# Another order, engine choice and slot choice for the same pieces of a rotary attention and squared-ReLU MLP kernel

## The chip, the cores and the metric

The kernel runs on one core of a Trainium2 chip. The metric is the device time of one execution in microseconds. Three executions of the kernel before took 625.17, 627.04 and 629.34 us, so the median is 627.04 us.

## The reference

There are 4 batches of 8 heads, 576 positions and 64 dimensions per head. Attention with a rotary embedding of q and k is followed by an MLP on 2304 tokens of width 512 with 2048 hidden units, all in float32:

```python
q_rot, k_rot = rotate(q), rotate(k)                 # rotary, halves of 32
scores = scale * np.matmul(q_rot, k_rot.transpose(0, 1, 3, 2))
scores = scores - np.max(scores, axis=-1, keepdims=True)
attn = np.exp(scores)
attn = attn / (np.sum(attn, axis=-1, keepdims=True) + 1e-09)
out = np.matmul(attn, v)                            # then (2304, 512)
h = x @ w_in
g = s * np.maximum(h, 0.0) ** 2 + b
return g @ w_out
```

## The kernel before

**Pieces.** The function `plan` writes the whole kernel down as 2657 pieces, each with the engines that may run it, the pieces it depends on and the buffers that it opens. Heads are handled in 16 pairs (`pr`, 0 to 15), each with nine score tiles of 128 queries by 576 keys (`i`, 0 to 8; tile 8 holds the last 64 queries of both heads). Tokens go through the MLP in nine units of 256 (`u`, 0 to 8); unit 8 collects the tails of all batches.

**The first pairs and unit 0.** Pairs 0 to 3 are computed in float32: `rotate` (three tensor_tensor steps per operand, lines 573 to 577), `qk_T` (PE transposes, lines 748 and 751), `s_pair` (scores, L638), `s_max` (DVE, L662), `s_exp` (ACT), `p_T` (L776), `pv32` (L795). Unit 0 uses float32 weights (`mlp_in0` L889, `mlp_out0` L906).

**The weights.** The host passes w_in and w_out as 64-bit words. Each of 32 blocks is loaded into one of four `x` slots (`load_w`, L419) and made into float32 by `w_sign`, `w_low`, `w_rebias` and `w_join` (lines 383 to 391). `w_gram` (PE, L459) finds their size, and `w_hi` and `w_lo` split them into two float16 halves. No unit above 0 can start before that.

**The other pairs and units.** Pairs 4 to 15 work with q, k and v split in float16 halves; q and k are transposed by DMA (`transpose_qk`). Probabilities are split by `p_a` (ACT, DVE or POOL: `pab<-p,sum`) and `p_b` (DVE, L388), transposed by DMA from the SP queue (`p_t`, L720, and `p_tt`, L724: `pt<-pab`), and multiplied with v in `pv_sum` (PE, L741, 28 matmuls). A unit runs 16 `mlp_in` (L863, 12 matmuls), `mlp_r` (ACT), `g_hi` (ACT or DVE), `g_lo` (DVE or POOL, L881), 32 `mlp_out` (L930, 3 matmuls), two `out_sum` (DVE) and a `store`. Unit 7 runs last.

**What sets the order.** Three strings do. ORDER is the sequence of all 2657 pieces, two characters for each; PICKS gives the engine of each piece that has a choice (S for ACT, V for DVE, G for POOL); SLOTS gives the buffer of each tile. Every engine runs its own pieces in the sequence of ORDER, every DMA is issued by SP in that sequence, and an engine whose next piece isn't ready waits, with all that stands behind it.

```python
order = [64 * DIGITS.index(ORDER[i]) + DIGITS.index(ORDER[i + 1]) for i in range(0, len(ORDER), 2)]
engs, where, at, steps = iter(PICKS), iter(SLOTS), {}, {}
```

The casts of `p_a`, `qk_hi`, `w_hi` and `v_hi` go through one helper (L383 on DVE, L385 on POOL, L391 on ACT), so in the rows they are told apart by their tiles.

Of the kernel before, what the change touches and what calls it, by code (L numbers as in the profile page):

```python
# [35 lines left out]


ORDER = (
    "AJDTAAEBDUAMAKALECDcDdEDDeEEDfEFEGDgANDhAdEAELEMENDiA3ADA5AfAgD_EHEIAEDjDkDlAeAhEJAFAGAHA6ESDpDqD1EKA4DrA9BAAOJjD2JkDsAI"
# [3 lines left out]
    "BOB2BfBPKJFTK6K7KKKCBhBgETBkEtBQBiFUBlBmB4EwLCBnKWKXBwKLKYKRKDKMKEB6LDB3KeCSBcBWLELFBoE4B5FVBdK8B-FhKSBpBjKfB7KTB8FQKgCV"
    "KZKaKbBqKhCBB_KnKvKwCUKiClLGKUKcKoKdKpCTCAKqKVCWKxCnCmCoKjLJKkK9CCKrCpKyLRLKB9KlCDCLCyCNCYLLLMKmCOKsLrEqK-CEKtLSLTLNLsLU"
    "KzLOC1LVCMCPbLbMbObNCZFHK_LHLtEUC0bPbQCbFKLICaLuLaCsCzLWK0LPCtExbRLicdEyEzbScebTCcE0cfcgE1chLjF7CuF-LkCvC2cicjLbLlE-MRCd"
    "CXLmLXLcLQLvCeE_CwLdMSLYC_CFDCDBLZDADDLnMTLeMUckLfCHLgFkbWbYbXbVLwbZbaE8L3KuK1CfF6DML4MEE9ChMVFRLxbgK2L5MFK3MWCiCIbfL0L1"
# [39 lines left out]
PICKS = (
    "GSSGVSGSSGGSGSSGSSGSSGSSGSSGSSGSGVSSGSSGSSGGGVSSGSSGSGVSSGVSVVSGSSVSSGSGGGSVVSGSSVVSVVSGSSGSSGSSVVSSSVVSSSVVSSSVVSSSVVSS"
    "SVVSGVGGSSSVVSGSVVSSGVVSGGVVSGSVVVSSVVSGSVVSGVVVVGVVGSSVSSSSSSSSSVVSSSSSSSSGSSGSSGVSSSVGSSSSVVSGSSSSVSSSSSVGSVSSSSSSSSSS"
    "SSSSSSSSSSSSSGSSSSSSSSGSGSSSSVSSVSVSSSSSSVSSVSSSSSVSSSSSSVVSSVVSSGSVSSVVVVSGVGSVSVVGVSVGVVVVSSVSSSSGVSGVVVSSSSVVSGSVSSSG"
    "SVSGSVSVSSSSSVVSSGVGVSSSVVSVGVSVSVGSVVSVSVVGSGGVVVSSGVVGSSGGGSGGGSVSGGSSGVSGSSGSVVGSGGSGSSSVVSVSGSGSVSGSVSVSSGSGSVSGSVSV"  # L90
    "SGSVSSVSGSVSGVVVVVVSVVVVVGSGSVVGSGSGSVVVGSGVVSGSVVVVGSVVVVSGVVVGVGSGSGSVVVVVGSGSGSGVVSGVVVSVSGVVSVVVSVVGSG"
)

SLOTS = (
    "000000111002311010000101010123100311110201012001011010030201001203001132100331100112100101013011020103032311001100310210"
    "021010011110010011013212203345120010103100300010001012211511001301013041010001122301100203010011311011500120012103001103"
    "041321001101134012011301202201030100011131301100110540021002011101132305121011011010020102030013011040250100300111121301"
    "100101330112303100041101050101020001234210115013100111230100014101005310120012100301010510020101121120101120310100104522"
    "301100001101110011020210011231100000421031012101103013101140101300223110002111102203023000103110031110050011020010402100"
    "010031110001312001150200410301310211021201011500011131200104020111110500030131010010112031001310141010252130000001121033"  # L100
    "021301001140111000215201110003310411113020031051112010102204001113112101211021300010025010301201402310000110131401100503"
    "011120131321100300420101013151120022014121100301010101120321011020201101001240021001110201113021001300151022201101302100"
    "1041110021010100001312104013100011001021010101013111010210100001112000010012000"
)


# [948 lines left out]
```

## Time and profile before

| what | value |
|---|---|
| median of three executions | 627.04 us |
| the profiled execution's own time | 627.53 us |
| its span, first to last instruction | 625.7 us |
| PE busy | 588.8 us, 94% of the span |
| DVE, ACT, POOL busy | 470.6, 407.3, 123.8 us |
| DMA queue 1 | 89.54 MB, 63.5% of 16 engines |

Busy time is the union of an engine's instructions. Durations of matmuls overlap, as the next one starts before the last has drained: three `mlp_out` matmuls last 0.81 us, and the next work starts 0.65 us after their beginning.

### The profile page before, as it was taken

The numbers are of one execution on the slowest core, as the hardware profiler recorded it, in microseconds if no ns is written. First come the engines' busy times: TensorE is split into PE (matmuls) and PEld (weight loads), VectorE is DVE, ScalarE is ACT, GpSimd is POOL, SyncE is SP. The second block draws the span as 40 slices with busy tenths as digits, with TensorE's granted clock in tenths as the row PEclk, the third lists the DMA queues.
The fourth block names the chain that finished last, engine by engine and source line by source line (L and its number), as shares of the span: only waits on it lengthen the run. The fifth ranks groups of instructions, "written<-read, shape, count | busy, mean of one in ns | idle before, by whom it ended". The sixth has DMA issues, their size and how long they took to land.

```text
span 625.7 us, 12358 instructions
## 1 busy us (share of the span) xinstructions
PE 588.8 (94%) x4634; PEld 396.5 (63%) x4634; DVE 470.6 (75%) x1029; ACT 407.3 (65%) x858; POOL 123.8 (20%) x127
## 2 busy tenths in 40 slices
...
GB/s 282 262 296 200 234 229 243 130 205 171 205 139 104 103 164 224 140 197 174 132 156 142 115 148 144 168 186 134 136 119 65 21 71 40 109 76 39 35 1 34
DMA packets 209868, 90.32 MB, mean 144 GB/s; under 512 B 192272, under 2 KB 196496, under 8 KB 209808
## 3 DMA queue, kind: packets, MB, share of 16 engines
q1 hardware_dynamic: 209808, 89.54, 63.5%
...
q14 instruction: 24, 0.20, 0.1%
...
## 4 chain that ended last, share of the span: by engine, by line
PE 73%; DMA 10%; DVE 7%; ACT 3%; issue 3%; SPq 2%; POOL 1%; DVEq 0%; ACTq 0%; POOLq 0%
PE px L863 25%; PE po L930 24%; PE px L741 8%; PE s L656 7%; DMA pt<-pab 5%; PE po L906 2%; PE px L889 2%; PE s L638 2%; DVE s L662 2%; DMA x<-in_moe_w_in_dram 2%; DMA x<-in_moe_w_out_dram 2%; DVE wio L388 1%; DMA qkT<-nat 1%; PE s L657 1%; ACT x L391 1%
## 5 line engine op out<-in xcount | busy, mean ns | idle before, releaser
L930 PE MATMUL po<-wio,g 128*128 128x512 f16 x768 | 185.5, 379 | 0.0
L863 PE MATMUL px<-xa,wio 128*128 128x256 f16 x1536 | 181.8, 273 | 0.0
L863 PEld LDWEIGHTS <-wio 128*128 128x128 f16 x1536 | 148.3, 98 | 32.8 <-issue 1.3
L391 ACT ACTIVATE p<-s,nm 128x576 f32<-128x576 f32 x144 | 105.6, 734 | 71.5 <-DVE s L662 50.8
L388 DVE SCALAR_TENSOR_TENSOR pab<-p,sum,pab 128x576 f16<-128x576 f32 x136 | 112.0, 839 | 7.3 <-POOL pab L385 4.9
L930 PEld LDWEIGHTS <-g 128*128 128x128 f16 x768 | 70.2, 98 | 73.3 <-issue 4.7
L662 DVE TENSOR_SCALAR_CACHE_REDUCE s<-s,sc 128x576 f32<-128x576 f32 x108 | 87.7, 820 | 24.7 <-PE s L657 22.3
L391 ACT ACTIVATE hr<-px,xc 128x512 f32<-128x512 f32 x64 | 43.6, 682 | 72.4 <-PE px L863 70.9
L881 POOL TENSOR_TENSOR g<-hr,g 128x512 f16<-128x512 f32 x31 | 39.0, 1257 | 189.5 <-ACT g L391 100.2
L391 ACT ACTIVATE pab<-p,sum 128x576 f16<-128x576 f32 x75 | 56.2, 766 | 9.8 <-DVE sum L690 8.0
L741 PE MATMUL px<-pt,v 128*64 128x320 f16 (+2 forms) x640 | 52.0, 281 | 7.2 <-DMA pt<-pab 6.7
L765 DVE CAST g<-hr 128x512 f16<-128x512 f32 x22 | 9.4, 428 | 51.2 <-ACT hr L391 48.2
L385 POOL TENSOR_SCALAR pab<-p,sum 128x576 f16<-128x576 f32 x26 | 23.4, 902 | 123.2 <-DVE sum L690 70.4
L741 PEld LDWEIGHTS <-v 128*64 128x64 f16 x640 | 35.6, 109 | 18.7 <-issue 13.0
L391 ACT ACTIVATE hr<-hr 128x512 f32<-128x512 f32 x68 | 42.7, 628 | 1.5
L656 PE MATMUL s<-qkT 128*128 128x512 f16 (+1 forms) x120 | 41.4, 383 | 0.0
L656 PE MATMUL s<-kS,qkT 128*128 128x512 f16 (+1 forms) x120 | 41.3, 380 | 0.0
L656 PEld LDWEIGHTS <-qkT 128*128 128x128 f16 (+1 forms) x240 | 21.9, 100 | 25.1 <-issue 5.0
L385 POOL TENSOR_SCALAR wio<-x 128x512 bf16<-128x512 f32 (+1 forms) x27 | 22.9, 859 | 54.5 <-ACT x L391 23.7
L889 PE MATMUL px<-x,wio 128*128 128x128 f32 x256 | 32.3, 279 | 0.0
L889 PEld LDWEIGHTS px<-x,wio 128*128 128x128 f32 x256 | 30.0, 192 | 3.1 <-issue 2.2
L662 DVE TENSOR_SCALAR_CACHE_REDUCE s<-s 128x576 f32<-128x576 f32 x36 | 26.8, 766 | 6.1 <-PE s L638 6.1
...
## 6 DMA issues: line engine op xcount, KB each, us to landing
...
```

What stands on the lines that cost most here:

```text
L385: eng.tensor_scalar(out=out, in0=in0, scalar1=s1, scalar2=s2, op0=op0, op1=op1)
L388: nc.vector.scalar_tensor_tensor(out=out, in0=in0, scalar=scalar, in1=in1, op0=op0, op1=op1)
L391: nc.scalar.activation(out=out, in_=in_, func=func, **kw)
L638: nc.tensor.matmul(ps[h][:, to], d["qF"][hh, t * P:(t + 1) * P], d["kF"][hh, keys], start=True, stop=True)
L656: nc.tensor.matmul(ps[rows, MAIN:2 * MAIN], lhs, kk[:, h:8:2], start=(n == 0), stop=(n == 1))
L662: nc.vector.tensor_scalar(out=T["s"], in0=T["s"], scalar1=-1.0 / 8.0 if pr in FQ else st[pr]["es"], scalar2=None, op0=ALU.mult, op1=ALU.mi ...
L741: nc.tensor.matmul(o[64 * h:64 * h + 64, c], v_rows(pr, h, k, z), p_rows(pr, 2 * (i // 4) + h)[:, k, c], start=((z, k) == todo[0]), stop=( ...
L863: nc.tensor.matmul(ph, w16[0][:, f, wz, cc], X["xa"][:, xz, c], start=(c == 0 and n == 0), stop=(c == NC - 1 and n == 2))
L881: (nc.vector if eng == DVE else nc.gpsimd).tensor_tensor(out=g[:, 1], in0=r, in1=g[:, 0], op=ALU.subtract)
L889: nc.tensor.matmul(ph, wi[:, f + 1, c * P:(c + 1) * P], xs[0]["x"][:, c, j * P:(j + 1) * P], start=(c == 0), stop=(c == NC - 1))
L906: nc.tensor.matmul(X["po"][:, j * DM:(j + 1) * DM], gs["h", j, f - f % 4][:, f % 4 * P:(f % 4 + 1) * P], wo[:, f + 1], start=(n == 1), sto ...
L930: nc.tensor.matmul(po, g[:, gz, jj], w16[1][:, f, wz], start=(n == 1 and i == 0), stop=(n == NF and i == 2))
```

## The change

The pieces, their dependencies and the code that emits them stay. ORDER, PICKS and SLOTS are replaced as a whole by strings of the same lengths, which come from a second search at a lower temperature that drew four sets of transfer delays at a time.

```diff
 ORDER = (
-    "AJDTAAEBDUAMAKALECDcDdEDDeEEDfEFEGDgANDhAdEAELEMENDiA3ADA5AfAgD_EHEIAEDjDkDlAeAhEJAFAGAHA6ESDpDqD1EKA4DrA9BAAOJjD2JkDsAI"
+    "AADTEBADDUEAD_AJDcDdECDEEDDeDfEFDiDgELDhEMAEEIENAFAMDjALA3AKANAdDkDlJjAGA5EJAHAfA6AeDrDpAgDsJkAhEGA4JlA9DqEHEKA7DtJrJsJt"
...
-    "GSSGVSGSSGGSGSSGSSGSSGSSGSSGSSGSGVSSGSSVSSGGGVSSGSSGSGVSSGVSVVSGSSVSSGSGGGSVVSGSSVVSVVSGSSGSSGSSVVSSSVVSSSVVSSSVVSSSVVSS"
...
```

Decoded, the first DMAs of SP are, before: `load_w(0,1)`, k of pair 0, rope table and identity, v of pair 2, q of pair 0, `load_w(0,4)`, q of pair 2, `load_w(0,8)`, `load_w(0,0)`, k of pair 2. After: rope table and identity, k of pair 0, v of pair 2, `load_w(0,0)`, q of pair 0, q of pair 2, k of pair 2, `load_w(0,1)`, `load_w(0,8)`, `load_w(0,4)`. The first pieces of DVE are `w_low(0,1)` and then the rotation of k of pair 0 before, and that rotation after.

PICKS moves these pieces (counts; all kinds not listed stay or move by one):

| kind | POOL | DVE | ACT |
|---|---|---|---|
| `w_sign` | 24 to 17 | 8 to 15 | - |
| `w_low` | 3 to 3 | 6 to 4 | 23 to 25 |
| `w_rebias` | 4 to 8 | - | 28 to 24 |
| `w_hi` | 15 to 13 | 4 to 4 | 13 to 15 |
| `v_hi` | 2 to 4 | 4 to 1 | 10 to 11 |
| `p_a` | 26 to 31 | 35 to 28 | 75 to 77 |
| `g_hi` | - | 22 to 25 | 42 to 39 |
| `g_lo` | 31 to 34 | 33 to 30 | - |

The last pieces of PE before are `mlp_out` of unit 7 with (f, j) = (14,1), (15,1), (14,0), (15,0), and DVE then runs `out_sum` for j = 0 and j = 1. After, they are (14,1), (14,0), (15,0), (15,1), with the same `out_sum` order. The last `g_hi` and `g_lo`, both on DVE before, are on ACT and POOL after; eight `mlp_out` stand between the last `mlp_in` and the first `mlp_out` that reads them.

## Rows read from the trace of the kernel before

**Rows 1.** Busy time by stretch, with granted clock, DMA share and GB/s.

```profile
0.00:25.00 25.00, 9.23 (x49) 5.64 (x49) 17.67 (x32) 8.78 (x14) 3.89 (x8) 1.00 0.81 289
...
25.00:50.00 25.00, 19.25 (x130) 13.86 (x129) 18.95 (x47) 20.58 (x42) 9.26 (x13) 0.85 0.78 264
...
32.35:42.60 10.25, 6.06 (x59) 4.21 (x57) 8.29 (x21) 9.73 (x20) 2.99 (x4) 1.00 0.89 299
...
42.60:56.20 13.60, 13.09 (x56) 9.28 (x58) 10.33 (x21) 10.67 (x24) 3.98 (x7) 0.50 0.63 212
...
60.00:178.00 118.00, 110.11 (x900) 76.48 (x898) 106.19 (x253) 97.44 (x217) 31.65 (x33) 1.00 0.91 199
...
178.00:478.00 300.00, 297.63 (x2448) 197.43 (x2445) 263.33 (x565) 217.47 (x467) 55.13 (x51) 1.00 0.74 148
...
478.00:620.60 142.60, 142.60 (x1052) 95.53 (x1050) 53.49 (x112) 54.57 (x99) 20.08 (x18) 1.00 0.18 44
```

**Rows 2.** PE's waits, 60 to 178 us, then 178 to 621: total, times, longest.

```profile
PE px L741 <- DMA pt<-pab: 4.5, 5, 1.5
...
PE px L741 <- DMA pt<-pab: 2.1, 3, 1.1
```

**Rows 3.** PE's timeline, 30 to 44 us: start, us, work, idle before.

```profile
30.19 0.61 PE L459 MATMUL px<-wio 128*128 128x128 bf16 x4
...
34.13 0.39 PE L459 MATMUL px<-wio 128*128 128x128 bf16 x4 [0.70 <-DVE wmx L462]
...
43.11 2.08 PE L776 MATMUL po<-dg,p 128*128 128x128 f32 x8 [1.28 <-ACT pt L391]
```

**Rows 4.** Timelines of DVE and PE over the first 15 us.

```profile
4.26 0.46 DVE L383 TENSOR_SCALAR wio<-x 128x512 uint16<-128x512 uint16 x1 [3.08 <-DMA x<-in_moe_w_in_dram]
...
7.84 0.76 DVE L573 TENSOR_TENSOR z<-st_k,tab 128x576 f32<-128x576 f32 x1 [3.12 <-DMA tab<-in_rope_dram]
...
8.76 0.72 PE L540 MATMUL px<-st_v 128*128 128x128 bf16 x5 [8.76 <-DMA st_v<-in_v_dram]
...
10.39 0.75 DVE L573 TENSOR_TENSOR z<-st_q,tab 128x576 f32<-128x576 f32 x1
...
14.03 1.27 DVE L575 TENSOR_TENSOR st_q<-st_q,tab 128x576 f32<-128x576 f32 x1
```

**Rows 5.** DVE's waits for POOL, 20 to 43 us, then 43 to 60.

```profile
DVE wio L388 <- POOL wio L385: 2.6, 3, 1.3
...
DVE wio L388 <- POOL wio L385: 1.3, 1, 1.3
```

**Rows 6.** Groups by line and form: busy us, mean ns, idle before.

```profile
L881 POOL TENSOR_TENSOR g<-hr,g 128x512 f16<-128x512 f32 x31 | 39.0, 1257 | 189.5 <-ACT g L391 100.2 <-DVE g L765 41.3 <-DVE sum L690 25.3
...
L881 DVE TENSOR_TENSOR g<-hr,g 128x512 f16<-128x512 f32 x33 | 24.3, 738 | 8.8 <-ACT g L391 8.5
...
L385 POOL TENSOR_SCALAR pab<-p,sum 128x576 f16<-128x576 f32 x26 | 23.4, 902 | 123.2 <-DVE sum L690 70.4 <-issue 18.0 <-DMA pt<-pab 14.0
...
L383 DVE TENSOR_SCALAR pab<-p,sum 128x576 f16<-128x576 f32 x35 | 18.4, 529 | 1.5 <-DMA pt<-pab 1.1
...
L388 DVE SCALAR_TENSOR_TENSOR wio<-x,wio 128x512 uint32<-128x512 uint32 x32 | 23.1, 724 | 4.4 <-POOL wio L385 3.7 <-issue 0.3 <-ACT wio L391 0.2
...
L662 DVE TENSOR_SCALAR_CACHE_REDUCE s<-s 128x576 f32<-128x576 f32 x36 | 26.8, 766 | 6.1 <-PE s L638 6.1
...
L383 DVE TENSOR_SCALAR wio<-x 128x512 uint16<-128x512 uint16 x14 | 6.5, 494 | 4.4 <-DMA x<-in_moe_w_in_dram 3.1 <-DMA x<-in_moe_w_out_dram 1.3
```

**Rows 7.** POOL's spread in the same two lines: min/median/max ns.

```profile
L881 POOL TENSOR_TENSOR g<-hr,g x31: 1152/1157/1778, 201.9 to 609.7; 128x512 f16<-128x512 f32 x31
...
L385 POOL TENSOR_SCALAR pab<-p,sum x26: 737/746/1362, 62.8 to 557.1; 128x576 f16<-128x576 f32 x26
```

**Rows 8.** Timeline of the end, 605 us on.

```profile
610.72 9.88 PE L930 MATMUL po<-wio,g 128*128 128x512 f16 x45
...
620.64 1.41 DVE L388 SCALAR_TENSOR_TENSOR o<-po,xc,bcs 128x512 f32<-128x512 f32 x2 [6.17 <-PE po L930]
```

More of the change, by code (lines that the diff above doesn't have):

```diff
@@ L43 @@
[L43 to L46, printed above, removed]
@@ L83 @@
-    "nznon3n4n5nqnyn0n6n8n-n7n9n_oAoBoC"
+    "AADTEBADDUEAD_AJDcDdECEDEEDeDfEFDiDgELDhEMAEEIENAFAMDjALA3AKANAdDkDlJjAGA5EJAHAfA6AeDrDpAgDsJkAhEGA4JlA9DqEHEKA7DtJrJsJt"
+    "DyA-DVAOAIEODuAPDvDwD1DxJuJmDWDXD2D3EPESEQBAAwAWDYJnDZAXA_DzBBJoEXEVAYJvAZD6AxAzD7ERAyD0A0AaEeAqArDaEYEZEfD4EWD5AtEaEhEb"
+    "DbAQJ0BCJpA8D8ATEsAjAmASAsEcAuEgARJ8ETJ1AlAkJ9J2J-DmBRBEJ3JqAUJ_AnBDEiEdBTBFBUEjEvE5ErBGABD9BrEkAiBSAoAvBHA1A2BIE6KAJ4Bt"
+    "BVEmElEnBxJwEoJxDnKFAVAbB0ByKNApKGBsBXEuJ5BzE2B1BYD-DoKHKOBZBaKIKJBbBuEpBKKPJ6J7BMFGBeFFFJBvK4BgKQBLK5AcBNBOE7JyK6KKBfLA"
@@ new lines @@
+    "KBBJBPJzKCLBB2BwBQK7FILCBhBkBWKLKWBcFTE3BiFULDB3BlEtBnBmEwKMKRB4KeKXKDLEB7B6CSLFKfKYBoB5E4KSKnFhB-BdK8FVKZKEB8KaKgKTFQCU"
+    "CVKhKvKbKUClKiK9CTKcCWBjBpB_CBKoKwKdCABqCCKpCoKqKxKjK-B9CDLJCEKrLKCmEqKkCnCpLLKlCLCNKsKyLRcdLrCYACKmLMLNKVKzCOCbLSLTKtLs"
+    "CMLULOLVbMbNbObLK_LGLtCabPLHLIbQLuCZCPCyFHCsC1C0EULWLPK0CcLacebRLiExEycfLvEzLjLkF7cgCtE0E1CuFKE-F-CzC2chLlLbbSbTCvCXCdCe"
+    "ciLmE_CwMRMSLnLXLQLYE8C_CFDBLcDCLdLeLwLZMTMUDADDLfCHLgbWbXbYbVbZbaFkK1KuL3MVL4MECfDMF6bgK2bfL5MFE9LxFRCIChCiF9K3L0MCbiL1"
@@ new lines @@
+    "MWcjbhbjDNCgL2CGbUbkCJbbCxC3MXGHGICjMDDPL6MGFSL7ckC4LhLoLpLqL_MdCQCKb2b0L8DOMHMeMAFAMIC5DGFfLyMBLzCRMqC6MfMLL9L-MMMJCkCq"
+    "M3bcb3M4CrMNMrMKFiC8M5C7M6clFLb1DHFMcmC9FNFOFPM7Fqb4b5M8MabdDEC-MbMoMcFYM9MgDQMhMpMlMsFWcncoMtMONANBNOFCMiMxMmDFFDMZFrDI"
+    "MuMvFXMjMybeb6b7blDRb8cpMQNPNCDJMPDKNDNQNENRNFNGNSMnF5MwMkMYMzFEFZNHNTcqbmbnbsNmDLbpbqbrN0DSNnNIF8NXNUNJNLNoFgbtbucrGVFa"
+    "FBM0FsGENVGFNYFcN1FjM1M2NdGGNeNMNfNgNhNicBFlcAb_Npb-NqFmN2FnNjNrNscCcDN3M_M-NKFdNZNNNWFtFuFvdDNtFoFecsboODbvdEbwb9cEN4Fp"
@@ new lines @@
+    "dFOEFwFyNxNuctN5GJFxNydGOFcuN9dHFzdINaOROGcFcJcGN6NccvF2NbN-OHcwOINvOSN7F_GAcIOUcLcKOJHJcxOKcyGTFbOVGBOTNzGUGYGXczOLGCGD"
+    "OMNlF3NwN8N_NkOkOWc0OlcMOOOPcNOXOYcHcUOhbxcOOiGWc1c2OcOZOdGhF4GiOmOjc3F0OAOyOzOaOCOBc4dwO0GMc5OeGvF1ONOvcScPdxbycQOwGKdy"
+    "dzc6d0OxOnOoO1d1d2c7bzO2d3d4OpGNGLd5cTcVP7O_cRd6eFeGcWO6HMc8GuOQObGQGRGtc9cXGjGec-P8c_eHOsdAdBOqOtdCO7GfeIO3d7d8P9d9cYcZ"
+    "d-dJdKeJd_O4eAdLPCOfOgeQcaGZcbPDdMdNGxGyPAP-ePGaPBccPEdOdPGwPFPQeBPNeDeCG7GbGcGgeKGddQPGPRPOP_GOGPO8OrO5OueRPHPKeSPSPIG4"
@@ new lines @@
+    "PLGSPPejPTQAPUdReLekelPdeZeEPgdSPYQBG8dTdUGkemGmPVeTeMO9eaeUdVGlPePfPZPhPiO-ebPjeceddWPWeOeNPueVdXdYGzPreXe4PvPsPkenPtPJ"
+    "PMPaHHPXdZG9daPlPwPxeoPyPodbG0G1dceee3efQHddQIG2P2e5e6PzeWeYQEehPbepdeerQFPpPmdfdgP3QGQJQKQLG3dhQSQTQUP0diQVegeteiQWQPHK"
+    "euQvPcQXQYdjfCQseqesPnPqP4P1GnHSQZHTQQe7QdQedkQwevewQtexQxGoHIeydldmdnP5QMQaP6QuQyHAdoQzQbHBe8Qje0eze1fBfOfPe2Q3fDfEfQQk"
+    "QlfRQNG5G6e-dpQ9Q6fAQmfSfTfUHLdqQRGpHjQDQcQfQCQOdre9e_fFfGQnQ-Q7Q0QoQ_Q4fVQ1fWQ8G-RAQpG_RBfXHiRFdsHlfIRXfHRzQgR0R1QifYHC"
@@ new lines @@
+    "dudtdvRYRCHUfZfaR2RDQhHvRGQ2Q5H7QrQqfbfcRZRURVHwfdfkHVRWRaRERHfJfjRlHNRiHOHPHQR3HRfKftfuHeRjRbfLfMHYfeR4HZHWRfRgRcRdR5fl"
+    "ffRkfhfmfnfofgfiRLRIRmHXRMHaH-fvRnfwRoHbRpRqIGfqR8fpf4R9fxRtRKfsRNRrHxfyR_SARJgLf3gMROGqR-SBHhHkSCSeRuRPIHSNfrfzf0f2H8HD"
+    "RhfNGrRvReSDRQRRSfH_gNRsf5IJRTRSIISOHsSgSEf6f7f8SKSFSLSHgOSPSIf1gBgPgQSMSQSRgCgDSbRwgEHmgFSVGsgGScSSSdHnf9Spf-f_gHShSWHo"
+    "RxRyHcHfH9SsgJgRgWgVgASGSJR7HpHqSTSiHrStSUR6SXSqHtSuSjSkHuIKHyHESrSvTHgIS5gfgKgXHzSwSxH0gYS0gZIAILgaSYgSgUgcH1H4SZSagsTI"
@@ new lines @@
+    "S6S1TJS7SmSygtgugvgggwgxgygzg0IWHFHdS8gegTgbSlIvH5g1S9g2SnS-ghgiIBTKTogdIZS_TLTAIjg4gjTMgkICH6H2S2SzSoH3g3TNg5TOTpIDIEIF"
+    "IMTBTCTSIyI6IOIPgmglgng6TlgohCTqhBTTg7gpg8S3TagqINTPhDTEhEHGTFg9g_g-TmTnS4TQhFTbhMhLTUhGTXIwTGIXTchghAhIT1TRTDIVI7I8TrhN"
+    "hOhPhQHgTshHhKTYTZTtT2TuTdTeTiTfIYTjIgT3TwT4hJTVTxIzTWT5hSTgT6UDUEhfhWhhhiT7T8UAhRIhhVUGhThphUhqUHUIgrT9TvTkUFhXhYhjUBhk"
+    "IkUJhZUKIlULUOhrIaU7U8U9U-hsIxThUPTyTzUTUUhaUVT0T-T_hbhdhlIbUMUNUCUQhtUfIchchehmhnVVUWUXUgU_huUhUYVWUZhoUcVXh0UqUdhzI9Ur"
@@ new lines @@
+    "IdUeVAUih1h2IeUthvhwVBUuUjIfUkh3UsIiUnI-UlUoh4URhxh-VSUSiKiLUvI0iMVTiNUwiOiPIQIoImh9h_iAVUIpUxiQiRiSiTVYiUh5hyh7h6h8VEVH"
+    "U1UyiBiCUmUpJKUbIRUzVZU2UaU0U3I_VFVIifiWiVigiDiFVJVGiXiYVjVaVdInWLVKJNVLVkVbiZihiiU4iaJXWMiEiGiIVeipISWNVMWOiHWPVlWQijVN"
+    "iqirisV9V6icieizJYikIqJJU6JMitITJLVcIUVmV7iuVPU5JOV8JUJViJi0ibidVOVDVfIrVCVvili-i9inimV-ioiwVQVRi1V_VnWAi2i3WBVoVwVpJWWF"
+    "WGi4WCVsVxi_jAivVgWlVtjBVuVyWDVzV3VhViV0WmWHWUWVVqV1V4V2VrWWWnJZjCWRjHjIiyI1WXWii6ixi5I2I3I4I5WYWZWaWbWjjRi7jSW8jJJCJAWf"
@@ new lines @@
+    "WkjKjLWEV5jTWcWgW9WdW-jUWzW0W1WIW_i8jcXyjEjDjMjFjNWoWpWtWuW2jbWeWTWSWhIsWJWqWrWsjVjWXAJDW3JGXBWvXCXzW4WKjdX0XNjGjOjeX1JP"
+    "jQjPWwJBXDXHXIX2XEXFW5ItIuX3X4X5jfX6XOJEJFWyWxjoXPXKjXXLXMXQjYjZjpX7jgjhjajijkXkjjXnjqjrjsXRJQjtjuJRjvjwJSjxjyXoXlJTXpXV"
+    "XSjlXTXWJckIkHjzj0JHXJW7W6XGXUXXkJkKkLkMXmJIXqXrj1X9Jaj2j9j-jmJgJdj_XvkAkBJbX-j3kCj4kSYDXbYEYFXYkRXcXdXeXwkTYGXfXgXhXaXZ"
+    "kUj6j5j8j7kEYdkvYakGkwJhJeX_XxjnkVYHXsXtYeXiX8XuXjYfYbYcYgZTZUZVYhYiJiJfYlYjYmkxYIYJkykDYMkFkNklYPkPYNYOYQYRYSYTYXYAZWZX"
@@ new lines @@
+    "kWkXZCkOkmYUYVZDZYYCZZZaYYZEZeknkzYKkQY3Y4Y0kYYnYkYZkakZk0ZfkoY5ZFkckbYLYWY1kpYBkqZGY2Y6Y7Y_ZAY8ZHkdZIY9keZJZKYrYok6k5a7"
+    "ZNYqYpYsZOkfYtYukgYvZLYwZkkhkikjkkkskukrktk1ZBY-a8YxZPZMk7k8ZlZmk9YyYzZQZRlGk-k3aCk_lHa9ZSoDk2k4lAlCZhlBoElIlJlKlLlMlNlO"
+    "lPlQoFlEoGoHoIoJoKoLlSlRlTlUlVlclbZilDoMldlWlelllmZja-lXlvlwlZlYa_ZnZoaDlnlolplflglhljmDlqlaZslxZplylzl0ZtZqZblilrlkl6l5"
+    "ltlslul1l2l3mEbAl7bBaEbCbGbHl8l9bDbEl-l_Z_l4mAmCmXmBmFmGmHmImJmYZcmZmaaAoNmOZxmKZyZzaBaFmNaGmPoOlFZumQZ0mRmSZrZgaKoPmLmb"
@@ new lines @@
+    "mcmTmMmVZ1Z2mUaSmWZ3Z4aHZ5Z6aTmeaUoQoRZdaLaIaPoZadmgZ8Z9ZvmdZwoYZ7aJaQaRmfawaeoaaVobaWZ-afocodmiaxmhaMmjoSaaoToiagojotoU"
+    "osahaiokolomabajakonaXaYalatoVoXaNouovoWoeo3auo2ofogohoporooaOamanacaoapaqaZo4avo5owo6oxayaza0a4o7a5a1a2ozo1o9arbIaspLpA"
+    "pBoqpKo_oyo0o8bFa6a3pCpDpEpFbJo-pHpMbKmkpNpOpVpGmlpPpJpIpUpQpSpRmmmnmompmqmrmsmtmupWpXpYpZm5m6pTpbpdmvm7m8m9m-pamwpcmxmy"
+    "mzm0nEnYnDpfpem2m1nFnGnHm4nXnNnOnIm3m_nPnQnRnSnBnJnLnTnAnCnKnVnZnanbncnhnsnMnUnWnrntndninfnupgnenjnvnwnknlnmn1ngn2nonqnn"
@@ L84 @@
+    "npn3n4nynxnzn0n5n6n8n7n9n-n_oAoBoC"
 )
 PICKS = (
[L87 to L90, printed above, removed]
```

63 lines of the change are left out of this document (14 added, 49 removed).

## The prediction

> **What bounds the kernel now.** I read busy time by stretch first, then PE's waits, then the timelines of the first 48 us and of the end. The stretches say where PE rests [rows 1]. From 478 to 620.6 us it never does. From 178 to 478 it rests 300 - 297.6 = 2.4 us, from 60 to 178 us 118 - 110.1 = 7.9. The first 50 us hold 25 - 9.2 = 15.8 and 25 - 19.3 = 5.8 us of rest, and after 620.6 us comes a tail of 5.1 us up to the end of the span at 625.7. So PE sets the pace from about 56 us on: a DVE that is busy 106.2 of 118 us matters only through PE's remaining holes.
>
> Those holes have one main cause: `pv_sum` waits for the DMA transposes of its probabilities, 4.5 us before 178 us and 2.1 us after [rows 2].
>
> Before 56 us two things count. The first is PE's clock. [...] Between 42.6 and 56.2 us the granted clock is 0.50 again [rows 1]. Ahead of that fall PE was busy only 6.06 of 10.25 us [rows 1], with waits such as 0.70 us, and it fell within a wait of 1.28 us [rows 3]. In the stretch PE was busy 13.1 of 13.6 us and got about half of that done, a loss of up to 13.6 x 0.5 = 6.8 us. The second is supply: PE does nothing until 8.76 us, when v has landed, and DVE is held by the rope table until 7.84 us [rows 4].
>
> **The change part by part.** No piece is added or dropped, so PE's matmuls cost what they cost. SP issues the same DMAs in another order, and SLOTS changes when a buffer comes free for the next load or tile; no row prices either by itself, so both stand in the bounds of the holes below. What can move is the start, the engines, the holes, the tail and the clock.
>
> *The start.* SP issues the rope table first; before, 512 KB of weights (128 x 512 words of 8 bytes) and 288 KB of k (128 x 576 of 4) stood ahead of it. At the 289 GB/s of the first stretch [rows 1] 512 KB are 1.8 us, so DVE's first rotation can begin near 6.1 us and not at 7.84 [rows 4] (k is needed too, and is now behind the table). The `w_low` of 0.46 us that DVE did at 4.26 us in its idle time [rows 4] goes to ACT. The second rotation needs q, and the bytes ahead of q are nearly the same in both orders: q can't land sooner than it did, which was between 8.76 us (v, just ahead of it) and 10.39 us (the rotation that used it) [rows 4]. So the gain lies between 0 and 1.6 us; I take 1.0, since q follows v closely in the queue.
>
> *Casts of the weights.* Seven `w_sign` go from POOL to DVE and two `w_low` from DVE to ACT, which is five more on DVE at 0.494 us [rows 6], 2.5 us. In return DVE's waits for POOL, 2.6 us from 20 to 43 us and 1.3 us after [rows 5], can go. The net is between -3.9 (the extra work falls into other idle time) and +2.5 us (the waits stay); ACT and POOL swap four `w_rebias` beside it, which I cost at nothing because both have idle time then. I take -0.5, because the waits go to ACT or DVE only in part.
>
> *Casts of the probabilities and of g.* Seven `p_a` leave DVE (0.529 us each), five of them for POOL (0.902), and three `g_lo` go from DVE (0.738) to POOL (1.257) [rows 6]. DVE is rid of about 7 x 0.53 + 3 x 0.74 = 5.9 us, less three more `g_hi`. None of this is on the path where PE has work queued, and after 178 us DVE has 36.7 us of slack in 300 (263.3 busy [rows 1]). Cover gone, each piece makes its reader later by the difference of the means, 5 x 0.37 + 3 x 0.52 = 3.4 us. I take nothing here, and the 3.4 for the range.
>
> *The holes of `pv_sum`.* Before 178 us they are worth between -4.5 (all gone) and, by as many new ones, +4.5 us. In the new ORDER seven and six PE pieces stand between the last transpose of pairs 2 and 3, second half, and the `pv_sum` that reads it, against five and none; the other pairs of the stage keep within two pieces of what they had. A place in ORDER is no time, so I take one fifth to one quarter, -1.0. After 178 us the bounds are -2.4 and +2.4; DVE, which writes what is transposed, has less to do, and I take -0.5.
>
> *The tail.* The last matmuls now end with j = 1, and j = 0 is complete one `mlp_out` earlier. That is 0.65 us (9.88 us for 45 matmuls in 15 pieces, less the drain [rows 8]). The two `out_sum` run one behind the other for 1.41 us after the last matmul [rows 8]; now the first overlaps it, a gain of 0.65 us. The last `g_lo` moves to POOL, slower by 0.52 us by the means [rows 6], and the last `g_hi` to ACT, but eight `mlp_out` of 0.65 us, 5.2 us, stand in front of their reader, so this is hidden.
>
> *Sum:* -1.0 - 0.5 - 1.0 - 0.5 - 0.65 = -3.65 us. The profiled execution took 627.53 us, 0.5 above the median of 627.04, so 623.9 against itself and 623.4 against the median. I predict 623.5 us.
>
> [...] POOL's `g_lo` takes 1152 ns at its shortest and 1778 at its longest, its `p_a` 737 to 1362 [rows 7], and a DVE rotation took 1.27 us in place of 0.75 [rows 4]. Both stretch at times, and a price at the longest rows, not at the means, is 7.3 us for the eight moved casts in place of 3.4 (worked out in rival 3). [...]
>
> **The rivals.** (1) *The clock doesn't fall.* If PE is fed well enough between 32 and 43 us, the half-rate stretch shortens or goes. DVE was busy 10.3 of those 13.6 us [rows 1], so it would allow 3.3 us at least, PE's own loss 6.8 at most; I take 5: 618.5 us. For it: the waits ahead of the fall are short, 0.70 and 1.28 us [rows 3], and the new order regroups that `w_gram` work. Against it: the same producers still feed PE. Chance 0.22.
>
> (2) *Slower: the clock falls a second time.* In the new order four `w_gram` (0,11), (1,1), (1,0), (0,12) all wait behind the same join: 18 DVE pieces follow the last one that PE needs for `p_T(1,0)`, among them five joins of 0.72 and three `s_max` of 0.77 us [rows 6], some 8 to 9 us in all. PE has five pieces for that time, each of about 1 us at full clock (`p_T`'s eight matmuls took 2.08 us at half clock [rows 3]). Before, the 15 DVE pieces of that distance were broken by two PE pieces that needed only part of them. [...] It decides as soon as the granted clock is 0.50 after 56 us. Chance 0.12, half of it beyond 1%.
>
> (3) *POOL's casts come late.* At their longest, eight moved pieces are 5 x 0.83 + 3 x 1.04 = 7.3 us later than on DVE, at their means 3.4 [rows 6, 7]: 627 to 631 us if PE waits for all. Against it: ample slack after 178 us. Chance 0.10, a third of it beyond 1%.
>
> (4) *Nothing gained:* holes move and keep their sum; 626 to 628 us. Chance 0.14.
>
> **How the numbers follow.** The forecast, 620.5 to 626, has 0.42. A measurement of this kernel tells about 1% from no change, so the bounds are 620.8 and 633.3 us. Faster: nearly all of rival 1 (0.20) and the low end of the forecast (0.06), 0.26. Slower: 0.06 of rival 2, 0.03 of rival 3, and 0.02 for holes that grow, 0.11. The rest, 0.63, is the same. The range of 616.5 to 631.5 takes in rival 1 with part of the other terms' lower bounds, rival 3, and the cheaper end of rival 2, and leaves out about 2 in 10.
>
> **What would show it.** DVE's first rotation near 6 us and `qk_T` soon after; fewer DVE waits for POOL before 60 us; PE's waits for transposes under 5 us in all; `out_sum` of j = 0 starting before the last matmul ends; a tail near 4.5 us. The granted clock between 32 and 60 us separates rivals 1 and 2 from the forecast. It would be wrong if PE rested more than 8 us between 60 and 178 us, or if a half-rate stretch stood later than 60 us.

## The result, and the profile after

The changed kernel took 619.34 us (median of four executions, 618.10 to 620.34) against 627.97 us for the kernel before in the same session: a ratio of 0.9867 [0.9826, 0.9908], 8.6 us or 1.4% less. That is under the 620.8 us from which the prediction speaks of faster, to which it had given 0.26, though the interval ends at 0.9% less; the 623.5 us that it named is 4.2 us too long, and 619.3 lies in its range. The profiled execution took 619.45 us, with a span of 617.5.

Busy time by stretch of the kernel after, for the stretches of [rows 1] (columns: length, then busy us of PE, PEld, DVE, ACT and POOL, granted clock, DMA share, GB/s). The last line is a stretch of its own.

```profile
0.00:25.00 25.00, 11.70 (x67) 8.04 (x68) 19.04 (x45) 11.18 (x20) 3.32 (x8) 1.00 0.84 309
25.00:50.00 25.00, 19.92 (x149) 14.30 (x149) 24.09 (x52) 21.28 (x45) 6.86 (x9) 1.00 0.85 271
32.35:42.60 10.25, 8.78 (x73) 6.71 (x70) 9.89 (x22) 8.70 (x19) 4.01 (x5) 1.00 0.89 268
42.60:56.20 13.60, 11.36 (x102) 8.45 (x102) 13.60 (x32) 13.14 (x34) 3.61 (x5) 1.00 0.82 273
60.00:178.00 118.00, 112.08 (x898) 78.83 (x897) 104.23 (x244) 99.78 (x220) 30.90 (x34) 0.99 0.90 199
178.00:478.00 300.00, 298.88 (x2450) 197.19 (x2449) 261.27 (x563) 213.91 (x457) 63.91 (x62) 1.00 0.72 144
478.00:612.40 134.40, 134.40 (x993) 90.02 (x990) 48.57 (x97) 54.07 (x98) 15.08 (x14) 1.00 0.22 48
...
114.10:117.50 3.40, 3.40 (x27) 2.88 (x26) 0.17 (x1) 0.21 (x2) 2.44 (x3) 0.50 0.00 0
```

Three things are new against [rows 1]. The half-rate stretch from 42.6 to 56.2 us is gone: the same 13.6 us hold 102 matmuls at clock 1.00 in place of 56 at 0.50, and DVE is busy all the time, 13.60 us in place of 10.33. PE does 67 matmuls in the first 25 us in place of 49. And a short half-rate stretch of 3.4 us stands at 114.1 us, where everything but PE and POOL nearly comes to rest (DVE 0.17, ACT 0.21, POOL 2.44, DMA 0.00).

The 1.00 at the start of such a table isn't a reading: the trace's record of the clock begins at 35.6 us here, and at 32.35 us in the trace of before. Four `w_gram` matmuls tell where PE was ahead of it: in the kernel before they take 0.40 us at 37.31 us, at a granted clock of 1.00, and 0.61 us at 50.34 us, at 0.50:

```profile
37.31 0.40 PE L459 MATMUL px<-wio 128*128 128x128 bf16 x4
...
50.34 0.61 PE L459 MATMUL px<-wio 128*128 128x128 bf16 x4
```

In the kernel after they take 0.61 us ahead of the record and 0.40 us behind its beginning, so PE was at half rate and then at the full clock:

```profile
33.49 0.61 PE L459 MATMUL px<-wio 128*128 128x128 bf16 x4
...
36.13 0.40 PE L459 MATMUL px<-wio 128*128 128x128 bf16 x4
```

So PE comes to the full clock some 3 us later than before (35.6 against 32.35 us), and then keeps it where the kernel before lost it (1.00 against 0.50 from 42.6 to 56.2 us).

The start, from DVE's and PE's timelines of the kernel after (start, us, work, idle before with its releaser); [rows 4] had 7.84, 10.39 and 8.76 us for these three:

```profile
5.53 0.76 DVE L573 TENSOR_TENSOR z<-st_k,tab 128x576 f32<-128x576 f32 x1 [4.36 <-DMA st_k<-in_k_dram]
...
8.55 0.76 DVE L573 TENSOR_TENSOR z<-st_q,tab 128x576 f32<-128x576 f32 x1 [0.52 <-DMA st_q<-in_q_dram]
...
6.33 0.71 PE L540 MATMUL px<-st_v 128*128 128x128 bf16 x5 [6.33 <-DMA st_v<-in_v_dram]
```

What DVE waited for between 25 and 60 us, before and then after (total us, times, longest):

```profile
DVE s L662 <- PE s L638: 3.1, 2, 2.8
DVE wio L388 <- POOL wio L385: 2.6, 3, 1.3
DVE mx L545 <- PE px L554: 0.8, 1, 0.8
```

```profile
DVE wio L388 <- POOL x L385: 0.6, 1, 0.6
DVE wio L388 <- ACT x L391: 0.3, 1, 0.3
```

Of 6.5 us 0.9 are left. The longest wait of before, 2.8 us for a score product, was DVE waiting for a PE at half clock.

PE's waits for transposes in the kernel after, from 60 to 178 us and then from 178 us on; [rows 2] had 4.5 and 2.1 us:

```profile
PE px L741 <- DMA pt<-pab: 4.8, 4, 1.9
...
PE px L741 <- DMA pt<-pab: 0.5, 2, 0.3
```

The end, from the timeline of the kernel after: both sums still follow the last matmul, and the tail is 617.5 - 612.4 = 5.1 us, as before [rows 1, 8].

```profile
604.47 7.93 PE L930 MATMUL po<-wio,g 128*128 128x512 f16 x36
...
612.44 1.41 DVE L388 SCALAR_TENSOR_TENSOR o<-po,xc,bcs 128x512 f32<-128x512 f32 x2 [9.54 <-PE po L930]
```

To place the gain, I priced each PE piece at its full-clock time and read, in each trace, when PE begins the piece that follows the same sum of such work. The table gives this time minus that of the kernel before (us; negative is ahead), at the times of before in its head. Every row is one execution.

| kernel | 8.8 | 53.3 | 64.7 | 84.7 | 112.9 | 127.4 | 190.0 | 265.8 | 297.9 | 615.9 |
|---|---|---|---|---|---|---|---|---|---|---|
| after | -2.4 | -6.4 | -5.7 | -6.1 | -6.3 | -3.7 | -6.8 | -6.9 | -8.3 | -8.2 |
| e1, new to 68 us | -2.0 | -5.5 | -3.8 | -1.2 | -1.1 | -1.4 | -2.1 | -0.3 | -0.2 | +0.6 |
| e12, new to 90 us | -1.9 | -6.5 | -4.0 | -4.7 | -4.2 | -4.8 | -4.2 | -3.0 | -3.5 | -3.6 |
| e8, new to 210 us | -1.6 | -6.0 | -5.3 | -6.0 | -6.6 | -6.3 | -8.7 | -7.7 | -7.9 | -7.4 |
| e9, new to 300 us | -0.6 | -5.2 | -4.5 | -5.2 | -7.0 | -6.2 | -9.0 | -9.4 | -10.5 | -9.2 |
| e2, old to 62 us | -0.6 | -0.6 | -0.1 | 0.0 | +0.1 | +0.8 | -0.3 | -0.1 | -1.4 | -0.4 |
| e10, old to 190 us | -0.8 | -4.1 | -3.7 | -3.2 | -2.9 | -3.4 | -2.5 | -2.9 | -4.4 | -4.1 |

The first column is PE's first matmul itself; behind it and ahead of 60 us a place is good to about one piece, 1 to 2.5 us. The first five rows have the same first 300 pieces, and yet their leads at PE's first matmul go from 0.6 to 2.4 us. Read in the same way at 37.3 us of before, none of the five is ahead by more than 1 us: the lead of the first matmul is gone there, and the 5 to 6.5 us at 53.3 us have come up since, in the time in which the kernel before ran at half rate.

### The profile page after: what moved, and what is told of

The parts are those of the page before. It is cut to its first block, busy times and chain, and to the rows that moved or that the text cites. A ratio compares the mean times of both kernels' runs of the same rounds, so it can differ in the third digit from the quotient of the medians.

```text
span 617.5 us, 12373 instructions
## 1 busy us (share of the span) xinstructions
PE 585.6 (95%) x4634; PEld 394.9 (64%) x4634; DVE 468.6 (76%) x1023; ACT 409.8 (66%) x860; POOL 123.7 (20%) x131
## 4 chain that ended last, share of the span: by engine, by line
PE 72%; DVE 10%; DMA 9%; ACT 4%; issue 3%; POOL 1%; SPq 0%; DVEq 0%; ACTq 0%; POOLq 0%
PE px L863 25%; PE po L930 23%; PE px L741 8%; PE s L656 7%; PE px L889 4%; DMA pt<-pab 3%; DMA st_k<-in_k_dram 3%; PE po L906 3%; DVE s L662 2%; DMA x<-in_moe_w_in_dram 2%; DMA x<-in_moe_w_out_dram 2%; ACT p L391 1%; PE s L638 1%; DVE pab L388 1%; DVE wio L388 1%
## 5 line engine op out<-in xcount | busy, mean ns | idle before, releaser
L388 DVE SCALAR_TENSOR_TENSOR pab<-p,sum,pab 128x576 f16<-128x576 f32 x136 | 115.1, 858 | 12.9 <-ACT pab L391 7.3
L881 POOL TENSOR_TENSOR g<-hr,g 128x512 f16<-128x512 f32 x34 | 41.7, 1225 | 203.9 <-ACT g L391 92.1
L391 ACT ACTIVATE pab<-p,sum 128x576 f16<-128x576 f32 x77 | 58.0, 765 | 6.9 <-DVE sum L690 4.8
L385 POOL TENSOR_SCALAR pab<-p,sum 128x576 f16<-128x576 f32 x31 | 27.1, 875 | 119.0 <-DVE sum L690 88.3
L391 ACT ACTIVATE hr<-hr 128x512 f32<-128x512 f32 x68 | 42.6, 627 | 1.4
L881 DVE TENSOR_TENSOR g<-hr,g 128x512 f16<-128x512 f32 x30 | 20.5, 687 | 17.6 <-ACT g L391 17.3
```

The source lines that it names most:

```text
L385: eng.tensor_scalar(out=out, in0=in0, scalar1=s1, scalar2=s2, op0=op0, op1=op1)
L388: nc.vector.scalar_tensor_tensor(out=out, in0=in0, scalar=scalar, in1=in1, op0=op0, op1=op1)
L391: nc.scalar.activation(out=out, in_=in_, func=func, **kw)
L881: (nc.vector if eng == DVE else nc.gpsimd).tensor_tensor(out=g[:, 1], in0=r, in1=g[:, 0], op=ALU.subtract)
```

## The experiments

The theory after the result: the start and the kept clock win about 6 us by 57 us, PE is the bound from there, and the lead is simply kept. The rivals: the clock alone; the rest of the order, without which the lead goes; the engines. In the three sessions of experiments the kernel before took 627.44, 627.67 and 627.63 us, and each time below was measured beside it.

**Cutting the order.** Six kernels join the two at a place; the first pieces of the base kernel are taken in the order, on the engines and in the buffers of the other one:

```diff
-ORDER = before                      # 2657 pieces
+ORDER = [n for n in after if n in before[:N]] + before[N:]     # e1: N=300, e12: 450, e8: 1050, e9: 1500
...
-ORDER = after
+ORDER = [n for n in before if n in after[:N]] + after[N:]      # e2: N=300, e10: 950
```

> The kernel before, with its first 300 pieces (to about 68 us) in the new order, on the new engines and in the new slots; all the rest as before. Theory A (the gain is won in the first 50 us, by feeding DVE and PE earlier, and kept because PE sets the pace afterwards): about 5.5 us faster than before, near 622, with DVE busy over 23 us between 25 and 50 us. Rival B (the gain is the half-rate stretch of 42.6 to 56.2 us that is gone): faster by about 5 only if the granted clock stays at 1.00 from 36 to 60 us, else nothing. Rival C (the gain lies in fewer holes after 60 us): 626 to 628, no change.

Measured: 626.06 us, ratio 0.9995 [0.9974, 1.0016]. The new start alone is worth little or nothing (1.4 us by the medians, 0.3 by the ratio), and the theory of a lead that is simply kept fell. In its trace the lead is there, 5.5 us, and goes in two steps. From 47.8 to 54.6 us the clock is at half rate (-5.5 to -3.8, and -2.1 for a while); behind the seam, -3.8 falls to -1.2. There ACT waits for weight loads, between 60 and 85 us in e1:

```profile
ACT x L391 <- DMA x<-in_moe_w_out_dram: 3.2, 1, 3.2
ACT wio L391 <- DMA x<-in_moe_w_out_dram: 2.1, 1, 2.1
```

and the chain of waits of e1 leads from two loads through ACT to PE (start, us, what):

```profile
62.16 4.99 DMA x<-in_moe_w_out_dram
...
67.23 0.70 ACT x L391
67.94 0.70 ACT p L391 x2
68.64 0.67 ACT wio L391
...
71.39 3.57 DMA x<-in_moe_w_out_dram
...
75.64 0.81 ACT p L391 x2
...
76.49 1.08 PE s L645 x4
```

The exponentials that PE needs stand on ACT behind casts whose weights haven't landed. PE is ahead, but what feeds it goes by the weight loads: it rests 1.7 us for `p` at 76.49. So up to 80 us a PE that is early doesn't stay early by itself.

> The changed kernel, with its first 300 pieces in the old order, on the old engines and in the old slots. Theory A: about 5.5 us slower than the changed kernel, near 625. Rival B: 625 if the granted clock falls to 0.50 between 40 and 60 us again, else 619. Rival C: stays near 619.

Measured: 623.95 us, ratio 0.9952 [0.9924, 0.9981]. The rest of the new order with the old start keeps 3.0 us by the ratio (627.44 x 0.0048) and 3.5 by the medians. Neither half alone gives the 8.6 us, and the two halves' gains don't add up to it.

> The kernel before, with its first 450 pieces (to about 90 us) in the new order, on the new engines and in the new buffers; the rest of the old. If the lead of the start was lost in the old order's stretch of 68 to 84 us, where VectorE, ScalarE and the weight loads still set the pace: TensorE comes out of it 5 to 6 us early and 622 to 623 us result. If what the first 300 pieces lost is lost again wherever the old order begins, or the gain of the first 1050 pieces comes from 90 to 210 us: 625 to 626 us.

Measured: 622.28 us, ratio 0.9917 [0.9892, 0.9942], 3.8 us less than e1 for 150 more pieces. ACT's longest wait between 60 and 85 us in e12, where those for loads are gone:

```profile
ACT p L391 <- DVE s L662: 1.7, 4, 0.6
```

and the stretch from 60 to 90 us, in e1 and then in e12: PE 25.51 against 28.08 us busy.

```profile
60.00:90.00 30.00, 25.51 (x260) 18.12 (x257) 25.97 (x73) 23.56 (x57) 8.95 (x11) 1.00 0.81 217
```

```profile
60.00:90.00 30.00, 28.08 (x283) 21.05 (x279) 26.83 (x75) 26.09 (x62) 8.71 (x12) 1.00 0.90 231
```

So the first expectation holds: the stretch behind 68 us is where the lead of the start was lost, and 5 us survive if the new order covers it.

> The kernel before, with its first 1050 pieces (to about 210 us) in the new order, on the new engines and in the new buffers; the rest of the old. If a lead is lost in one place, the old order's stretch from about 236 to 300 us (the transposes behind the stores and behind DVE's chain there): the lead is some 6 us until then and gone after it, 625 to 627 us, no better than the first 300 pieces alone (626.1). If the gain is spread evenly over everything behind 60 us: about a third of it, 623 to 624 us. If the start alone had made it, with a run of the old order spoiling it early: 620 us.

> The kernel before, with its first 1500 pieces (to about 305 us) in the new order, on the new engines and in the new buffers; the rest of the old. If the one place is 236 to 300 us: the lead passes it and is kept to the end, 619 to 621 us, as the kernel after. If the gain is spread evenly over everything behind 60 us: under half of it, 623 us. If another hole of the old order lies behind 305 us, which only a kernel that comes early would meet: 624 us or more, and its chain of waits names the hole.

Measured: e8 621.33 us, ratio 0.9910 [0.9883, 0.9938]; e9 618.70 us, 0.9880 [0.9853, 0.9906]. e8 lies between its expectations and meets none; e9 is just under its first. The idea that the lead is lost in the old order's stretch of 236 to 300 us fell with e8, which keeps 6 us through it. But 2.6 us lie between the medians of the two kernels (the intervals overlap), and PE's waits between 225 and 310 us differ by as much: in e8 the two below, in e9 and in the kernel after none.

```profile
PE px L741 <- DMA pt<-pab: 2.5, 3, 0.9
PE po L930 <- DVE o L388: 0.3, 1, 0.3
```

Behind 305 us old and new order give the same time (e9 618.70, after 619.34).

> The kernel after, with its first 950 pieces (to about 190 us) in the old order, on the old engines and in the old buffers; the rest of the new. If the gain is made before 210 us, in the start and then between 60 and 210 us: at most 1 to 2 us are left of it, 625 to 627 us. If the rest of the new order gains by itself, as the 4.6 us seemed to say that the kernel after lost with an old start: 623 to 624 us.

Measured: 625.44 us, ratio 0.9959 [0.9939, 0.9978], as the first expectation had it: about 2 us come from behind 190 us. Its profile shows more than it was made for. This execution has the old start, and its half-rate stretch is short, 33.3 to 36.7 us; in the stretches of [rows 1] it reads

```profile
32.35:42.60 10.25, 7.66 (x57) 5.45 (x57) 8.11 (x19) 9.82 (x21) 3.93 (x5) 0.83 0.78 283
42.60:56.20 13.60, 10.95 (x89) 7.33 (x88) 13.60 (x29) 12.80 (x31) 5.74 (x7) 1.00 0.79 262
```

with DVE busy throughout, as in the kernel after, and it leads by 3.7 us at 64.7 us. The same old start with a clock that falls (e2) leads by 0.1. So in these two executions the shorter fall goes with 3.6 us at 64.7 us, and the kernel after is 2.0 us sooner still (-5.7). Other traces widen this. e3, with the old start but for one load and a half-rate stretch of 3.4 us only (43.1 to 46.5), leads by 1.3 us at 64.7 us. Of the new start, e12 and e7 have 3.4 us at half rate between 54 and 60 us and lead by 4.0 and 2.8 us; after, e6, e8, e9 and e11 have none between 38 and 60 us and lead by 4.5 to 5.7. So at a like fall the new start is worth 1 to 3 us at 64.7 us, and the new start doesn't always keep the clock.

**The clock.** In the kernel before, 60 matmuls of 384 columns whose results nothing reads are added around the first ten `w_gram` of the input weights:

```diff
+        if n == 1:        # and the same behind the group where n == 2
+            for c in more:   # 6 where which == 0 and f < 10
+                nc.tensor.matmul(wst["g", which, f // 2][:, P:4 * P], w[:, 0:P], w[:, P:4 * P], start=True, stop=True)
```

> The kernel before with sixty more matmuls of 384 columns, whose results nobody reads, six beside each of the first ten w_gram pieces; they fill PE's waits between 30 and 43 us so that the clock has less reason to fall, and cost about 0.16 us each at full rate. Rival B: the granted clock stays at 1.00 to 60 us and the time falls by some 3 us, to 624. Theory A: even with the clock at 1.00 the time doesn't fall, 627 to 631, since DVE is not fed earlier and PE has 10 us more to do, most of it inside waits. If the clock falls all the same, nothing is told.

Measured: 624.83 us, ratio 0.9976 [0.9956, 0.9996]. PE does more, and the kernel is shorter by 1.5 us by the ratio (627.44 x 0.0024; 0.3 to 2.8 by its interval) and 2.6 by the medians. The expectation's 0.16 us for each is an estimate; at the 7.93 us for 36 matmuls of 512 columns at the end of the kernel after, one of 384 is 7.93 / 36 x 384 / 512 = 0.165 us. In e4's trace the clock falls earlier and not at 42.6 us:

```profile
23.30:33.60 10.30, 8.86 (x52) 6.20 (x53) 8.70 (x24) 7.31 (x17) 4.32 (x5) 0.50 0.67 225
33.60:42.60 9.00, 8.62 (x67) 5.56 (x66) 6.02 (x16) 7.28 (x16) 2.40 (x3) 1.00 0.80 267
42.60:56.20 13.60, 12.56 (x96) 8.42 (x95) 10.86 (x23) 10.92 (x24) 5.09 (x6) 1.00 0.67 223
```

Its expectation would tell nothing if the clock fell all the same. It did, at 23.3 us, but there PE was at half rate in the kernel before too (0.61 us for the four matmuls at 30.19 us [rows 3]), and the fall of 42.6 us is gone. So a clock that stays up there is worth something like 2 us of time in the old order, extra work included, and not the 8.6.

**The start's first load.** In the kernel before, the rope table is put first in the order:

```diff
-ORDER: load_w(0,1), k of pair 0, table, v of pair 2, ...
+ORDER: table, load_w(0,1), k of pair 0, v of pair 2, ...
```

> The kernel before with one piece moved: the load of the rope table and the identity is issued ahead of the first weight block. Theory A, with the start as its larger part: DVE's first rotation near 5.5 us in place of 7.8 and 2 us off the end, near 625.5. Theory A, with the engines as its larger part: the 2 us are lost again at the first weight block, which lands later; no change, 627. Rival B: no change unless the clock's fall goes with it.

Measured: 627.30 us, ratio 1.0007 [0.9987, 1.0028]. In its trace the first rotation begins at 8.01 us and PE's first matmul at 8.78. The table was not what the start waited for: as long as the 512 KB of weights stand ahead of k and v, these land no sooner.

**The engines.** e5 is the kernel before with the new engines for its first 300 pieces (ten `w_sign` from POOL to DVE, five `w_rebias` from ACT to POOL, and eleven more); e6 is the kernel after with the old engines for the 203 pieces outside its first 300 whose engine differs.

```diff
-PICKS = before
+PICKS = [after[i] if i in ORDER[:300] else before[i] for i in pieces]      # e5 on before, e6 on after
```

> The kernel before, with the new engines for the pieces among its first 300; order and buffers stay the old. If the order makes the start: VectorE keeps some 5 us of waits between 25 and 60 us and the time is 626 to 629 us. If the weight casts that leave GpSimd make it: VectorE's 2.6 us of waits for GpSimd go, TensorE is 2 to 3 us early at 60 us, and the time is 624 to 625 us.

> The kernel after, with the old engines for every piece outside its first 300; order and buffers stay the new. If the order is what keeps the lead: 619 to 620 us, as the kernel after. If the engines of the late pieces (copies that go to ScalarE or to GpSimd instead of VectorE) are what keeps it: 623 us or more, with TensorE waiting for the copies that were moved.

Measured: e5 632.14 us, ratio 1.0072 [1.0050, 1.0094], 4.5 us slower than the kernel before; e6 639.81 us, 1.0201 [1.0172, 1.0229], 20.5 slower than the kernel after. e5 is beyond both of its expectations, and e6 meets the second, by far more than it said. In e5 DVE's waits for POOL go from 2.6 to 0.5 us, as wished, but PE waits up to 3.2 us for DVE's `wmx`, with a half-rate stretch from 50.3 to 63.9 us in this execution. In e6 PE waits between 60 and 600 us as below, 18.2 us in these six lines; the kernel after has 6.7 us in all (5.2 for transposes, 0.6 and 0.4 for `p`, 0.5 for `pt`), which leaves some 7 of the 18.3 us between the two spans unexplained:

```profile
PE s L656 <- ACT p L391: 5.8, 7, 1.8
PE px L741 <- DMA pt<-pab: 3.9, 5, 1.0
PE po L930 <- DVE g L881: 2.4, 1, 2.4
PE po L776 <- ACT pt L391: 2.2, 1, 2.2
PE px L828 <- ACT g L391: 2.1, 2, 1.7
PE px L557 <- DVE wmx L462: 1.8, 1, 1.8
```

The old engines are good in the old order and cost 20 us in the new one: in these two mixes order and engines are one choice, and neither has a price of its own. The buffers went with the order in both and weren't tried apart.

**The tail.** e7 puts the last unit's first sum ahead of the last group of matmuls; e11 also gives that half a PSUM tile of its own.

```diff
-mlp_out(7,15,0), mlp_out(7,15,1), out_sum(7,0), out_sum(7,1)
+mlp_out(7,15,0), out_sum(7,0), mlp_out(7,15,1), out_sum(7,1)
...
+        if u == 7 and j == 0:        # e11 alone
+            X["po0"] = ps_s.tile([P, 1024], F32, tag="s0", name="s0", bufs=1)
+            po = X["po0"][:, 0:DM]
```

> The kernel after, with the last tile's first output sum put ahead of the last group of output matmuls in the order, so that it waits for matmuls of its own half alone. If the sum may run beside the last matmuls once the order says so: it starts about 0.7 us before the last matmul ends, and the tail of 5.1 us is 0.6 to 0.7 us shorter, 618.7 us. If the two halves lie in one buffer whose last writer is what the sum waits for: tail and time as in the kernel after, 619.3 us.

> The kernel after, with the last tile's first half accumulated in a PSUM tile of its own, and its output sum put ahead of the last group of output matmuls. If the shared tile is what joined the two halves: the sum runs beside the last three matmuls, TensorE no longer stops 0.84 us in front of them, and one sum of 0.75 us follows the last matmul in place of two (1.41 us): 618.6 us, 0.65 under the kernel after. If the sum is held by something else: 619.3 to 620 us, with the sum behind the last matmul.

Measured: e7 618.78 us, ratio 0.9869 [0.9841, 0.9897]; e11 617.22 us, 0.9844 [0.9817, 0.9871], the shortest median here, though its interval overlaps that of the kernel after. The end of e7, and then of e11 (its tiles are `s` and `po`):

```profile
614.06 0.75 DVE L388 SCALAR_TENSOR_TENSOR o<-po,xc,bcs 128x512 f32<-128x512 f32 x1 [8.89 <-PE po L930]
...
614.86 0.81 PE L930 MATMUL po<-wio,g 128*128 128x512 f16 x3 [0.84 <-DVE o L388]
...
615.71 0.75 DVE L388 SCALAR_TENSOR_TENSOR o<-po,xc,bcs 128x512 f32<-128x512 f32 x1 [0.90 <-PE po L930]
```

```profile
609.16 0.81 PE L936 MATMUL po<-wio,g 128*128 128x512 f16 x3
609.36 0.75 DVE L388 SCALAR_TENSOR_TENSOR o<-s,xc,bcs 128x512 f32<-128x512 f32 x1 [8.89 <-PE s L936]
610.03 0.74 DVE L388 SCALAR_TENSOR_TENSOR o<-po,xc,bcs 128x512 f32<-128x512 f32 x1
```

With one tile, the sum waits for the matmuls ahead of it and PE then stands 0.84 us for the sum: the order moves the wait and doesn't end it. With two tiles the sum runs beside the last three matmuls, and from the last matmul's end (609.16 + 0.81) to the end of the span at 614.5 there are 4.5 us, 0.6 less than in the kernel after. The other 1.5 us of the 2.1 between the medians of e11 and after aren't explained by the tail; they were measured in different sessions, and e11's profiled execution had no fall of the clock at 114 us.

## Why the prediction was right or wrong

The range held the time and the forecast pointed the right way, but its sum of 3.65 us was too small: the start was mis-sized, the tail's term failed, PE was taken as the bound too early, and the time is nearer to rival 1 than to the likeliest case. That it lies in the range is in part luck: the gain is not made of the terms of the sum.

**The start** (-1.0) measured -2.3 us at the first rotation, -1.8 at q's and -2.4 at PE's first matmul in the profiled execution; e9, with the same start, has -0.6 at that matmul and is no slower. It isn't a term of the time either, as the lead is gone at 37.3 us. The bound of 1.6 us assumed that q can't land before v did at 8.76 us; but v itself landed 2.4 us sooner, because no weights stand ahead of it. I had given the gain to the table, and e3 shows that it belongs to the 512 KB of weights behind the table.

**Casts of the weights** (-0.5). DVE's waits for POOL did go, to 0.6 us. That this has a price of its own was wrong: the same engines in the old order cost 4.5 us (e5).

**Rival 1, the clock** (0.22, 618.5 us) named nearly the time that came, 619.3, and what it describes is in the trace: PE is fed better ahead of the fall (73 matmuls against 59 in the 10.25 us [rows 1]), the clock stays at 1.00 there, and DVE's long wait for PE goes. Its price of 5 us is not shown. At 64.7 us a shorter fall goes with 3.6 us by e10 against e2 and with 1.3 us by e3, one execution each, and how much of it shows in the total depends on the rest of the kernel: 1.5 to 2.6 us in the old order (e4), where a lead is lost behind 60 us. So it is a term that I left out of the forecast, of some 1 to 4 us at 64.7 us, and the nearness of 618.5 is in part luck. What else in the new start makes the 1 to 3 us beside it wasn't separated; its engines alone don't (e5).

**A step that the prediction didn't have:** it took PE as the bound from 56 us on, so that a lead is kept. e1 shows that it isn't, up to about 80 us; the new order holds it there (e12), and that is as necessary as the start. In the trace of before PE came to that place later and rested only 0.8 us for the same `p`, so the hole couldn't be read off as one of PE's.

**The holes from 60 to 178 us** (-1.0). PE's waits for transposes didn't shrink, 4.8 us against 4.5. The reading of ORDER held where it was made, for the second halves of pairs 2 and 3, before and then after:

```profile
150.78 0.98 PE L741 MATMUL px<-pt,v 128*64 128x320 f16 x10 [1.40 <-DMA pt<-pab]
166.75 0.84 PE L741 MATMUL px<-pt,v 128*64 128x320 f16 x9 [1.50 <-DMA pt<-pab]
```

```profile
146.98 0.87 PE L741 MATMUL px<-pt,v 128*64 128x320 f16 x9 [0.96 <-DMA pt<-pab]
```

What it had wrong is that the other places would stay. The first half of pair 2 now waits 1.59 us in place of 0.49, and the second half of pair 0 waits 2.2 in place of 0.72:

```profile
84.77 0.47 PE L741 MATMUL px<-pt,v 128*64 128x128 f16 x10 [1.59 <-DMA pt<-pab]
...
114.04 1.45 PE L741 MATMUL px<-pt,v 128*64 128x320 f16 x9 [1.88 <-DMA pt<-pab]
```

The lead grows from 5.7 to 6.8 us between 64.7 and 190 us all the same, after a loss of 2.6 at 114 us.

**Rival 2** (0.12) came in small. Its cheaper price was an estimate, 13.6 x 0.5 = 6.8 us on top of the 623.5 us, from the half-rate stretch of before [rows 1]; no run shows it, and 3.4 us at half rate cost about 2 us. The clock did fall behind 56 us, for 3.4 us, but not at the `w_gram` join. It fell at the `pv_sum` that had waited 1.88 us for a transpose, with PE busy 0.22 us between 112.0 and 114.1. The lead shrinks by 6.3 - 3.7 = 2.6 us there. e8 and e9 have the same pieces up to there and wait 1.59 and 1.71 us at the same place, but their clock doesn't fall, and their leads shrink by 0.3 and 0.8 us; so the fall itself cost about 2 us in that execution, near the 3.4 x 0.5 = 1.7 us of PE's own work. What makes the clock fall isn't shown: here it fell behind a wait of 1.88 us for a transfer, in e8 and e9 it didn't behind 1.59 and 1.71 us for the same one, and the wait of 1.28 us at the fall of 42.6 us before was for ACT and not for a transfer [rows 3]. By the prediction's own words a half-rate stretch behind 60 us would have made it wrong; it was one stretch of 3.4 us and not of 13.6.

**The holes after 178 us** (-0.5): the waits for transposes go from 2.1 to 0.5 us, and the lead grows by 1.4. Right in kind, and worth 2.6 us between e8 and e9.

**The tail** (-0.65) failed: 5.1 us as before. I took the first sum to depend on its own half alone. Both halves are one PSUM tile, and e7 and e11 show that the tile joins them; with two tiles the 0.6 us are there.

**Rival 3, POOL's casts late** (0.10), didn't come. The medians of POOL's two lines, 1158 and 748 ns, are within 2 ns of those of [rows 7], with longest ones of 1669 and 1757, and PE waits for no POOL piece between 60 and 600 us. What makes them so long, no run here shows. It decided nothing.

**Open:** why the clock falls in some executions of one kernel and not in others, and so how much of the 8.6 us it is in a given one. Of the kernel before, 14 executions with a mean granted clock of 0.996 or more had a median of 627.1 us and 21 below 0.992 had 628.2; of e2, 3 had 623.2 and 6 had 626.8 (at 0.991 or less). But this mean counts the time ahead of the first record as full rate: the 0.989 of e9's profiled execution is a half-rate stretch from 22.9 to 36.5 us with none behind it before the tail, and the fastest execution of the kernel after, 618.10 us, has 0.985. So without a trace the mean can't tell a fall at 42.6 us from a slow start.
